# Forward and backward of a recurrent-memory transformer block: hand-laid buffers in one tile and stages that hand over inside each other's last steps

## The chip, the cores and the metric

The kernel runs on one core of a Trainium2 chip. The metric is the device time of one execution in microseconds (us). A core has five engines, each with its own instruction queue worked off in order: TensorE (PE, with its weight loads PEld), VectorE (DVE), ScalarE (ACT), GpSimd (POOL) and SyncE (SP). In this kernel SP does nothing but start DMAs, and POOL starts DMAs beside a few copies. An instruction can wait for events of other engines and of DMAs; everything behind it on its engine then waits too.

## The reference

A block with 2048 tokens of width D = 448 is computed, and the gradients of all its inputs. The attention part walks through 64 segments of 32 tokens in order; each segment also carries 8 memory rows, and the memory rows of its output are the next segment's memory, so that segments depend on each other.

```python
mem = mem0
for s in range(n_seg):                                  # 64 segments of 32 tokens
    h = concatenate([mem, x[32 * s:32 * s + 32]])       # 8 + 32 rows
    q, k, v = h @ Wq, h @ Wk, h @ Wv                    # 16 heads of 256
    p = softmax(where(mask, q @ k.T / 16, -1e9))
    o = (p @ v) @ Wo
    mem = o[:8]; outs.append(o[8:])

h  = x + attention(layernorm(x))
h2 = h + (silu(n @ w_gate) * (n @ w_up)) @ w_down       # n = layernorm(h), inner width F = 1792
out, vjp = jax.vjp(block, x, mem0, Wq, Wk, Wv, Wo, w_gate, w_up, w_down)
return out, *vjp(grad_out)
```

All inputs and outputs are bfloat16; sums are float32 in PSUM.

## The kernel before

Four stages run one after the other, each a function that issues its instructions in the order in which they are to run; the order within each engine's queue is the order of the code.

1. `forward_chain` (from L406): 64 steps, one for each segment, about 14.0 us each. A step projects K, Q and V (L471, L479), transposes K and Q (L485), computes scores, softmax and PV (L516 to L814) and the output projection (L600), and hands the memory rows to the next step. V's rows are moved to other partitions by copies or by DMAs on SP (`v_shift`; L667 is the DMA form). Beside its own segment a step works at a side task for the row tile of 128 tokens (four segments): `u1`, `u2`, `u3` are PE work, `e1`, `e3` evictions, `ut` a transpose, `et` the last reduction. In the last step `ff.load_first` asks for the gate and up weights (L895, L897, on POOL).
2. `ffn_phase`: 16 row tiles of 128 tokens, forward and backward of the FFN. `gate`, `up` and `dz` are products with the gate, up and transposed down weights (L996, L999), `down_mm` is L1050, `dh_mm` L1079; `turn_f`, `hn_turn`, `dout_turn` and `dh_out` are transposes on PE; `slope` and `grads` are DVE work, `dh_ln` is the LayerNorm gradient (DVE). `ff.load_rest` (L905 to L911) asks SP for the down weight, its transpose `WdT` and the transposed gate and up weights. The shape 448 is three and a half times 128: WdT's last DMA transpose takes the last 128 columns, and a further DMA (L909) copies their second 64 rows to the first 64 partitions. A steady tile takes 20.2 us.
3. `backward_chain`: 64 steps in the opposite order, about 14.6 us each: gradient of the outputs through Wo (L1191), scores' gradient (L1472 to L1482), outer products (L1494), products with the transposed V, K and Q weights (`w_pass`, L1218). `load_back` (L926) loads such a transposed weight by one DMA transpose on SP.
4. `tail_phase`: 22 phases of weight gradients. p = 0 and 1 (L1674) use `GO_all`, p = 2 to 5 `HN_all` (L1689), p = 6 to 21 the attention's weights. A phase's large operand is loaded two phases ahead (`load_phase`), from p = 6 on by 16 DMA transposes on SP (L1629). In the first two phases memory rows are loaded, transposed and stored again (`mem_turn`, L1657 to L1666).

The weights lie in one SBUF tile `Wall` of four parts; each stage places its own weights there. All other buffers come from tile pools that are opened and closed with their stage: `workA`, `stageA`, `wfwd` for the first, `workB`, then `workC`, `stageC`, then `tailA`, `workD`. A pool's space is given to the next stage's pools. PSUM has eight banks: stages 1 and 3 use six in rotation and two fixed ones, stages 2 and 4 eight in rotation (`psf` is a bank used as float32, `psh` as bfloat16).

Of the kernel before, what the change touches and what calls it, by code (L numbers as in the profile page):

```python
# [18 lines left out]
class _Prio:  # L19
# [5 lines left out]
    def crit(self):  # L25
        from contextlib import contextmanager

        @contextmanager
        def _cm():
            off = self.tc.cur_priority - self.next  # L30
            with self.tc.high_priority(offset=off):
                yield
                self.next = self.tc.cur_priority
        return _cm()

# [147 lines left out]
def run_all(k: _K):  # L183
# [89 lines left out]
    with tc.tile_pool(name="wfwd", bufs=1) as wf, \  # L273
            tc.tile_pool(name="psA", bufs=6, space=bass.MemoryType.PSUM) as psa, \
            tc.tile_pool(name="psS", bufs=1, space=bass.MemoryType.PSUM) as pss:
        k.pspool = psa
        k.s_ps = [pss.tile([P, 512], FP32, name=f"s_ps{i}") for i in range(2)]
        for i in range(2):
            nc.vector.memset(k.s_ps[i][:], 0.0)
        Wk_sb, Wq_sb, Wv_sb = [W[i].rearrange("p (c n) -> p c n", c=KC) for i in range(3)]  # L280
        Wo_sb = W[3][:, 0:MC * D].rearrange("p (c d) -> p c d", c=MC)
        NWIN = 8
        hA = wf.tile([P, KC, NWIN, SEG], BF16)
        memT_all = W[3][:, MC * D:KC * HD].rearrange("p (c s m) -> p c s m", c=KC, s=NSEG)
        k.memT_all = memT_all
        maskf = wf.tile([L, L], FP32)
        nc.gpsimd.memset(maskf[:], 0.0)
        nc.gpsimd.affine_select(out=maskf[:], in_=maskf[:], compare_op=ALU.is_ge, fill=-1e9 / k.scale,
                                base=0, pattern=[[-1, L]], channel_multiplier=1)
        nc.gpsimd.memset(maskf[0:M, :], 0.0)  # L290
        maskr = wf.tile([L, H // 2 * L], BF16)
        for hh in range(H // 2):
            nc.vector.tensor_copy(out=maskr[:, hh * L:(hh + 1) * L], in_=maskf[:])
        k.part = wf.tile([P, DP], FP32, name="part")
        k.partB = wf.tile([P, DP], FP32, name="partB")
        nc.vector.memset(k.part[:], 0.0)
        nc.vector.memset(k.partB[:], 0.0)

        with tc.tile_pool(name="workA", bufs=2) as work, tc.tile_pool(name="stageA", bufs=1) as stage:
            order = ExitStack()  # L300
            order.enter_context(tc.manual_schedule())
            DB = D // 4
            m0f = work.tile([P, DP], BF16, name="m0", tag="xtmp", bufs=2)
            m0 = m0f[0:M, :]
            nc.sync.dma_start(out=m0[:, 0:D], in_=MEM0)
            Xs = W[3][:, 0:NT * D].rearrange("p (t d) -> p t d", t=NT)
            XNs = W[3][:, NT * D:2 * NT * D].rearrange("p (t d) -> p t d", t=NT)
            xv = X2.rearrange("(t p) d -> p t d", p=P)
            xnv = XN.rearrange("(t p) d -> p t d", p=P)
            for q in range(4):  # L310
                nc.sync.dma_start(out=Xs[:, 4 * q:4 * q + 4, :], in_=xv[:, 4 * q:4 * q + 4, :])
            for Wt, Wsrc in ((Wk_sb, Wk2), (Wq_sb, Wq2), (Wv_sb, Wv2)):
                wv = Wsrc.rearrange("(a j p) n -> a p j n", a=2, j=2)
                for a in range(2):
                    nc.sync.dma_start(out=Wt[0:DB].rearrange("p (j a) n -> p j a n", a=2)[:, :, a, :], in_=wv[a])
            pm = ps1(BF16)
            for kc in range(KC):
                w0 = (kc % 2) * 2 * DB + (kc // 2) * DB
                nc.tensor.transpose(pm[0:DB, kc * M:(kc + 1) * M], m0[:, w0:w0 + DB], ident[0:M, 0:M])
            k.evac(hA[0:DB, :, 0, 0:M], pm[0:DB, 0:KC * M].rearrange("p (c m) -> p c m", m=M), "v")  # L320
            nc.scalar.copy(out=memT_all[0:DB, :, 0, :], in_=hA[0:DB, :, 0, 0:M])
            mv1 = small.tile([P, NT, 2], FP32, name="mv1", bufs=1)
            sd1 = small.tile([P, NT], FP32, name="sd1", bufs=1)

            def norm_rows(out, t):
                nc.vector.tensor_scalar(out=out, in0=Xs[:, t, :], scalar1=mv1[:, t, 0:1], scalar2=rstd1[:, t:t + 1],
                                        op0=ALU.subtract, op1=ALU.mult)

            def first_rows(t):
                xl = work.tile([P, DP], BF16, name="xload", tag="xload", bufs=1)  # L330
                norm_rows(xl[:, 0:D], t)
                return xl

            def norm_group(q):
                ts = range(4 * q, 4 * q + 4)
                for t in ts:
# [7 lines left out]
            def store_group(q):  # L344
                for t in range(4 * q, 4 * q + 4):
                    norm_rows(XNs[:, t, :], t)
# [60 lines left out]
def forward_chain(k: _K, hA, NWIN, Wq_sb, Wk_sb, Wv_sb, Wo_sb, maskr, work, stage, ff):  # L407
# [289 lines left out]
    for s in range(NSEG):  # L697
# [44 lines left out]
        if s == NSEG - 1:  # L742
            ff.load_first()
# [186 lines left out]
def ffn_phase(k: _K, W, ff, work, mv2, rstd2, srcs):  # L930
# [194 lines left out]
    for t in range(NT):  # L1125
        if t + 2 < NT:
            load(t + 2)
# [715 lines left out]
```

## Time and profile before

| | us |
|---|---|
| median of three runs (lowest to highest) | 3011.68 (2999.15 to 3012.10) |
| profiled execution | 3027.69 |
| its span, first to last instruction | 3025.9 |

The median comes from runs without the profiler; the profile is of another, single execution. Its page gives first the busy time of each engine and its share of the span, and then the span in 40 slices, each digit a tenth of busy time, with PE's granted clock and the DMA engines' share under it:

```profile
PE 2782.4 (92%) x44584; PEld 1532.9 (51%) x44584; DVE 1527.2 (50%) x3995; ACT 1175.6 (39%) x3087; POOL 737.2 (24%) x1388
...
PE   3999999999997899977999999999997999989998
...
PEclk7999999999999899987999999999998999999999
DMA  9334434334335853377556655655666999999996
```

A slice is 75.6 us. The forward stage fills slices 1 to 12, the FFN 13 to 17, the backward stage 18 to 30, the tail the rest. Two fives in the DMA line mean that the mean DMA engine was busy half of that slice.

### The profile page before, as it was taken

The numbers are of one execution on the slowest core, as the hardware profiler recorded it, in microseconds if no ns is written. First come the engines' busy times: TensorE is split into PE (matmuls) and PEld (weight loads), VectorE is DVE, ScalarE is ACT, GpSimd is POOL, SyncE is SP. The second block draws the span as 40 slices with busy tenths as digits, with TensorE's granted clock in tenths as the row PEclk, the third lists the DMA queues.
The fourth block names the chain that finished last, engine by engine and source line by source line (L and its number), as shares of the span: only waits on it lengthen the run. The fifth ranks groups of instructions, "written<-read, shape, count | busy, mean of one in ns | idle before, by whom it ended". The sixth has DMA issues, their size and how long they took to land.

```text
span 3025.9 us, 104914 instructions
## 1 busy us (share of the span) xinstructions
PE 2782.4 (92%) x44584; PEld 1532.9 (51%) x44584; DVE 1527.2 (50%) x3995; ACT 1175.6 (39%) x3087; POOL 737.2 (24%) x1388
## 2 busy tenths in 40 slices
PE   3999999999997899977999999999997999989998
PEld 1555555555554355544555555555554454444454
DVE  3566666666665577754555666555663111112121
ACT  2444445454453466543444444444542011111110
POOL 1222222222222122211222322222222223222231
PEclk7999999999999899987999999999998999999999
DMA  9334434334335853377556655655666999999996
GB/s 262 116 119 134 122 120 141 119 116 143 116 118 170 191 154 124 112 178 176 145 147 174 175 142 149 193 153 144 181 160 239 280 214 203 207 191 192 202 199 105
DMA packets 623699, 494.03 MB, mean 163 GB/s; under 512 B 486144, under 2 KB 535888, under 8 KB 613696
## 3 DMA queue, kind: packets, MB, share of 16 engines
q1 hardware_dynamic: 574848, 295.48, 44.5%
q0 software_dynamic: 48384, 191.85, 19.5%
q8 instruction: 352, 5.77, 0.8%
q14 instruction: 115, 0.94, 0.1%
HBM read 137.63 MB, written 222.08 MB: 119 GB/s over the span
## 4 chain that ended last, share of the span: by engine, by line
PE 71%; DVE 8%; DMA 7%; issue 6%; ACT 4%; SPq 2%; POOL 1%; another core or an unknown queue 0%; POOLq 0%; ACTq 0%; DVEq 0%
PE psf L1689 12%; PE psf L1218 9%; PE psf L471 8%; PE psf L1191 5%; PE psf L600 4%; PE psf L996 3%; PE psf L1494 3%; PE psf L1674 3%; PE psf L479 2%; PE psf L1079 2%; PE psh L485 2%; PE psf L1702 2%; PE psf L814 2%; DMA V_sb<-Vev 2%; DMA wall<-in_A_Wv_dram 1%
## 5 line engine op out<-in xcount | busy, mean ns | idle before, releaser
L1689 PE MATMUL psf<-wall,H_all 128*128 128x512 bf16 x1440 | 325.8, 384 | 15.4 <-DMA wall<-dKA 10.3
L471 PE MATMUL psf<-wall,hA 112*32 112x512 bf16 x4096 | 234.6, 381 | 3.5
L1689 PEld LDWEIGHTS <-H_all 128*128 128x128 bf16 x1440 | 140.2, 99 | 184.7 <-issue 29.9
L1601 DVE CAST resc<-psf 128x512 bf16<-128x512 f32 (+1 forms) x58 | 39.1, 673 | 324.7 <-PE psf L1689 290.6
L471 PEld LDWEIGHTS <-hA 112*32 112x32 bf16 x4096 | 104.4, 97 | 113.8 <-DVE hA L529 12.9
L1599 ACT CAST resc<-psf 128x512 bf16<-128x512 f32 (+1 forms) x54 | 31.0, 573 | 337.1 <-PE psf L1689 299.7
L1545 POOL COPY dmem<-dA 128x32 bf16<-128x32 bf16 x63 | 13.2, 210 | 558.9 <-DVE dA L1230 558.9
L437 POOL COPY V_sb<-Vev 32x512 bf16<-32x512 bf16 x128 | 77.2, 603 | 273.9 <-ACT Vev L434 270.2
L1182 DVE COPY partC<-psf 128x224 f32<-128x224 f32 x64 | 25.1, 392 | 227.1 <-ACT partC L1185 227.1
L1191 PE MATMUL psf<-wall,dA 128*32 128x512 bf16 x2048 | 123.7, 384 | 13.0 <-DVE dA L1230 13.0
L479 PE MATMUL psf<-wall,hA 112*32 112x512 bf16 x2048 | 134.0, 382 | 0.0
L1674 PE MATMUL psf<-dOut_all,wall 128*128 128x448 bf16 x640 | 127.3, 357 | 6.5 <-DMA wall<-OTA 6.5
L1674 PEld LDWEIGHTS <-wall 128*128 128x128 bf16 x864 | 84.4, 99 | 95.2 <-issue 13.2
L1218 PE MATMUL psf<-wall,dkA 128*32 128x448 bf16 x2048 | 116.9, 371 | 14.6 <-DMA wall<-in_A_Wk_dram 12.1
L1218 PE MATMUL psf<-wall,dqA 128*32 128x448 bf16 x2048 | 112.1, 359 | 14.9 <-DMA wall<-in_A_Wq_dram 10.4
L1218 PE MATMUL psf<-wall,dvA 128*32 128x448 bf16 x2048 | 124.3, 362 | 0.9 <-issue 0.6
L1182 DVE COPY dO_sb<-dOev 32x512 bf16<-32x512 bf16 x256 | 120.4, 470 | 7.0
L600 PE MATMUL psf<-wall,oA 128*32 128x224 bf16 x4096 | 115.3, 267 | 0.3
L1185 ACT CAST dOev<-psf 128x512 bf16<-128x512 f32 x64 | 37.4, 585 | 184.8 <-PE psf L1191 181.0
L1218 PE MATMUL pob<-wall 128*32 128x448 bf16 x1536 | 107.3, 359 | 1.1 <-issue 1.1
L1185 ACT CAST wall<-psf 128x64 bf16<-128x64 f32 x512 | 106.7, 247 | 0.0
L600 PEld LDWEIGHTS <-oA 128*32 128x32 bf16 x4096 | 97.0, 99 | 8.1
(285 smaller groups left out, 5803.9 us busy)
## 6 DMA issues: line engine op xcount, KB each, us to landing
Vtok<-V_sb SPq DMA_DIRECT2D x128, 192.0 KB
KtokA<-Kev SPq DMA_DIRECT2D x64, 256.0 KB
QtokA<-Qev SPq DMA_DIRECT2D x64, 256.0 KB
OTA<-oA POOLq DMA_DIRECT2D x16, 1024.0 KB, 5.4
Q_sb<-QtokA SPq DMA_DIRECT2D x128, 128.0 KB
K_sb<-KtokA SPq DMA_DIRECT2D x128, 128.0 KB
dVA<-dvA POOLq DMA_DIRECT2D x16, 1024.0 KB, 5.8
dKA<-dkA POOLq DMA_DIRECT2D x16, 1024.0 KB, 7.8
```

The lines of the kernel that those rows point to most:

```text
L437: nc.gpsimd.tensor_copy(out=out, in_=in_)
L471: nc.tensor.matmul(ps[32 * g:32 * g + 32, :], lhsT=stat(kc), rhs=W_sb[0:DB, kc, c0:c0 + HB], start=(kc == 0), stop=(kc == KC - 1))
L479: nc.tensor.matmul(ps[32 * g:32 * g + 32, :].rearrange("t (y d) -> t y d", y=2), lhsT=stat(kc), rhs=wv[:, x, :, half, e, :], start=(kc == ...
L600: nc.tensor.matmul(ps[32 * g:32 * g + 32, 0:2 * DB], lhsT=x, rhs=Wo_sb[:, c, a * 2 * DB:(a + 1) * 2 * DB], start=first, stop=last)
L996: nc.tensor.matmul(out[b][:, 0:BW], lhsT=xT[:, kc, :], rhs=Wx[:, kc, f0:f0 + BW], start=(kc == 0), stop=False)
L1182: nc.vector.tensor_copy(out=out, in_=in_)
L1185: nc.scalar.copy(out=out, in_=in_)
L1191: nc.tensor.matmul(ps[32 * g:32 * g + 32, :], lhsT=stat(kc), rhs=WoT_sb[:, kc, c0:c0 + HB], start=(kc == 0), stop=(kc == KC - 1))
L1218: nc.tensor.matmul(pO[32 * g:32 * g + 32, 0:D], lhsT=ch(c), rhs=WT[:, c, :], start=(first and i < 4), stop=(last and i >= MC - 4), skip_gr ...
L1494: nc.tensor.matmul(po[:, n * L:(n + 1) * L], lhsT=lhs[b:b + L, lc:lc + P], rhs=rhs[b:b + L, hh, 0:L], start=True, stop=True)
L1674: nc.tensor.matmul(ps[:, 0:D], lhsT=stat[:, i, c * P:(c + 1) * P], rhs=Y[:, i, 0:D], start=(i == 0), stop=(i == kts - 1))
L1689: nc.tensor.matmul(ps[:, 0:N], lhsT=Hx[:, i, dc * P:(dc + 1) * P], rhs=X[:, i, b * N:(b + 1) * N], start=(i == 0), stop=(i == kts - 1))
```

## The change

Five things change; the diff leaves out what is only indented anew.

- One SBUF tile of 77,824 bytes a partition, the arena, takes the place of all stage pools. Four texts (`FWD`, `FFN`, `BWD`, `TAIL`) give each buffer its offset and its number of copies; a stage's `tile()` returns a view and takes the copies in turn. An instruction then waits only for those that touch the same bytes.
- One PSUM pool of six rotating banks and two fixed ones (`k.fix`) stays open throughout. The FFN's `down_mm` and `dh_mm` use the fixed ones.
- The FFN, backward and tail functions become generators. `next(feed)` in the forward stage's last step runs the FFN up to its next `yield`, `next(back)` in the FFN runs a part of the backward stage's start, `next(tails)` in the backward stage's last step the tail's first loads.
- In the forward stage's last step the three V shifts by DMA become copies on ACT and POOL. `load_rest` asks for WdT's transposes ahead of the down weight; the copy of the 64 odd rows goes to POOL.
- The FFN takes its last two row tiles in the order 15, 14, with their work interleaved; the transposed V, K and Q weights are loaded in two pieces each. sg, u and z get two copies; `slope` writes its result over sg.

```diff
+class _Stage:
...
+    def tile(self, shape, dtype, name=None, tag=None, bufs=None):
+        tag = tag or name
+        offs = self.slots[tag]
+        i = self.count.get(tag, 0)
+        self.count[tag] = i + 1
+        off, nb = offs[i % len(offs)]
...
+        return self.arena.view(off, shape, dtype)
+ARENA = 77824
...
+FFN = """h_ld:896x3 hn:1024x3 dout_ld#2:1024x2 dh_t:1792 lnb_prod:1792 lnb_t1:1792 dh_b:896 o_t:896x2 dT:1024x2
+dout_ld#0:1024x2
+du:3584 dgp:3584 dz:3584 scr:3584
+sg#0:3584 g#0:3584 u#0:3584 sg#1:3584 g#1:3584 u#1:3584
+doutT:1024x2
+z:3584x2 hnT:1024x2"""
...
 def run_all(k: _K):
...
+    arena = _Arena(wtp.tile([P, ARENA // 2], BF16, name="arena")[:, :])
+    fwd, ffn, bwd, tail = [_Stage(arena, ARENA, text) for text in (FWD, FFN, BWD, TAIL)]
+    k.pspool = ctx.enter_context(tc.tile_pool(name="psA", bufs=6, space=bass.MemoryType.PSUM))
+    pss = ctx.enter_context(tc.tile_pool(name="psS", bufs=1, space=bass.MemoryType.PSUM))
+    k.fix = [pss.tile([P, 512], FP32, name=f"s_ps{i}") for i in range(2)]
...
+        tails = tail_phase(k, tail)
+        back = backward_chain(k, WT, bwd, bwd, rstd1, dmem0T, tails)
+        feed = ffn_phase(k, WT, ff, ffn, mv2, rstd2, {"o": Wo2, "v": Wv2, "k": Wk2, "q": Wq2}, back)
+        forward_chain(k, hA, NWIN, Wq_sb, Wk_sb, Wv_sb, Wo_sb, maskr, fwd, fwd, ff, feed)
         nc.gpsimd.dma_start(out=memTd[0:DB], in_=memT_all[0:DB].rearrange("p c s m -> p c (s m)"))
+        next(feed)
+        for _ in back:
+            pass
+        for _ in tails:
+            pass
...
 def forward_chain(k: _K, hA, NWIN, Wq_sb, Wk_sb, Wv_sb, Wo_sb, maskr, work, stage, ff, feed):
...
-        nc.sync.dma_start(out=dr["Hh"][t * P:(t + 1) * P, :], in_=h_t)
+        eng = nc.gpsimd if t == NT - 1 else nc.sync
+        eng.dma_start(out=dr["Hh"][t * P:(t + 1) * P, :], in_=h_t)
...
         v_b_rows(s, V_sb)
+        final = s == NSEG - 1
+        if final:
+            next(feed)
...
-        v_shift(V_sb, Vev, 0, (2, 3), D_)
+        v_shift(V_sb, Vev, 0, (2, 3), A if final else D_)
...
-        v_shift(V_sb, Vev, 1, (0,), D_)
+        v_shift(V_sb, Vev, 1, (0,), G_ if final else D_)
...
         p_ev(1, 1, V)
+        if final:
+            next(feed)
...
             nc.sync.dma_start(out=dr["Vtok"][s, gg], in_=V_sb[QB * gg:QB * gg + 48, :])
+        if final:
+            next(feed)
...
         late["ut"]()
+        if final:
+            uo = o_units(t)
+            uo["u1"]()
+            uo["u2"]()
+            uo["u3"]()
+            next(feed)
...
+    uo["e3"]()
+    next(feed)
+    uo["ut"]()
+    uo["et"]()
+    next(feed)
     out_pe(NT - 1)
     out_ev(NT - 1)
...
     def load_rest(self):
...
-        nc.sync.dma_start(out=self.Wd, in_=Wd2.rearrange("(c p) d -> p c d", p=P))
         for kc in range(full):
             nc.sync.dma_start_transpose(out=self.WdT[:, kc, :], in_=Wd2[:, kc * P:(kc + 1) * P])
         nc.sync.dma_start_transpose(out=self.WdT[:, full, :], in_=Wd2[:, D - P:D])
-        nc.sync.dma_start(out=self.WdT[0:rem, full, :], in_=self.WdT[P - rem:P, full, :])
+        nc.sync.dma_start(out=self.Wd, in_=Wd2.rearrange("(c p) d -> p c d", p=P))
         nc.sync.dma_start_transpose(out=self.WgT, in_=k.aps["B_w_gate"])
         nc.sync.dma_start_transpose(out=self.WuT, in_=k.aps["B_w_up"])
...
     def down_mm(t):
-        T[t].pf = ps1(FP32)
+        T[t].pf = k.fix[0]
...
-    def dh_mm(t):
-        T[t].pdh = ps1(FP32)
+    def dh_mm(t, parts=range(2)):
+        pdh = k.fix[1]
...
+    ORD = list(range(NT - 2)) + [NT - 1, NT - 2]
+    HC = k.MC // 2
     load(0)
     load(1)
-    ff.load_rest()
+    yield
     rstd(0, NT - 1)
     norm(0)
-    rstd(NT - 1, NT)
-    norm(1)
+    yield
+    ff.load_rest()
+    yield
     hn_turn(0)
-    gate(0)
+    yield
+    gate(0, (0,))
+    nc.gpsimd.dma_start(out=ff.WdT[0:rem, full, :], in_=ff.WdT[P - rem:P, full, :])
+    yield
+    gate(0, (1,))
+    yield
+    norm(1)
     up(0)
     dout_turn(0)
     hn_turn(1)
     slope(0)
...
+    for i in range(NT - 2):
+        t, n1, n2 = ORD[i:i + 3]
...
+        if i == NT - 6:
+            next(back)
...
+        if i == NT - 3:
+            dout_turn(n1)
+            hn_turn(n2)
+            gate(n2)
+            load_back(k, WT["v"], srcs["v"], False, 0, HC)
+            up(n2)
+            load_back(k, WT["v"], srcs["v"], False, HC, 2 * HC)
+            dh_turn(t)
+            slope(n1)
+            slope(n2)
...
+        dh_mm(t)
+    p, q = ORD[NT - 2:]
+    turn_f(T[p].z, ff.zT, (A, A))
+    dz(p)
+    dh_ln(p - 2)
+    down_mm(p)
+    grads(p)
+    dh_out(p - 2)
+    down_ev(p)
+    dout_turn(q)
+    turn_f(T[q].z, ff.zT, (A, A))
+    dz(q)
+    load_back(k, WT["k"], srcs["k"], False, 0, HC)
+    down_mm(q)
+    down_ev(q)
+    next(back)
+    load_back(k, WT["k"], srcs["k"], False, HC, 2 * HC)
+    dh_turn(p)
+    grads(q)
+    dh_mm(p)
+    dh_ln(p)
+    dh_turn(q)
+    dh_mm(q, (0,))
+    dh_out(p)
+    next(back)
+    load_back(k, WT["q"], srcs["q"], False, 0, 14)
+    dh_mm(q, (1,))
+    load_back(k, WT["q"], srcs["q"], False, 14, 2 * HC)
+    dh_ln(q)
+    yield
+    dh_out(q)
+    yield
...
 def backward_chain(k: _K, WT, work, stage, rstd1, dmem0T, tails):
...
+    load_vT(NSEG - 1)
+    load_vT(NSEG - 2)
+    yield
+    nc.vector.memset(S_ps[:], 0.0)
+    kq = load_kq(NSEG - 1)
+    Pn = load_P(NSEG - 1)
+    yield
     nc.gpsimd.memset(dA[:, :, slot(NSEG - 1), 0:M], 0.0)
     new_tile(NT - 1)
     open_tile(NT - 1)
     nc.gpsimd.memset(tiles[NT - 1].dmem[:, :, 3, :], 0.0)
     fill_tile(NT - 1)
+    yield
     u = do_units(NT - 1)
...
-            cur = w_units(t + 1, "v") if t + 1 < NT else none_units()
+            cur = w_units(t + 1, "v") if t + 1 < NT else dict(none_units(), u2=lambda: next(k.feed))
...
+            eng = nc.gpsimd if s == NSEG - 1 else nc.sync
...
         outer(K_sb, dST, dqA, T.dW["q"], (V, A, V, A))
+        if s == 0:
+            next(tails)
...
 def tail_phase(k: _K, work):
...
     load_rows(GO_all, GO2, 4)
+    yield
     load_phase(0)
     load_phase(1)
-    load_rows(HN_all, dr["HN"], 1)
...
             for i in range(NG):
                 box = {}
                 at(i, lambda box=box, m=mems[p * NG + i]: box.update(pe=mem_turn(*m)))
-                at(i + 2, lambda box=box: box["pe"]())
+                at(i + 3, lambda box=box: box["pe"]())
+        if p == 0:
+            HN_all = work.tile([P, NKT, D], BF16, name="HN_all", tag="h2")
+            load_rows(HN_all, dr["HN"], 1)
```

The memory tiles of `mem_turn` have five copies instead of two. `dh_out` of row tile 14 writes straight into the buffer that the backward stage reads, without a store and a load.

745 lines of the change are left out of this document (380 added, 365 removed).

## The prediction

> **What bounds the kernel now.** I read the stretches first: the whole span cut at the points where one stage hands over to the next. Columns: stretch, its length, busy time (instructions) of PE, weight load, DVE, ACT, POOL, then the granted clock, the DMA share and GB/s.
>
> ```profile
> 62.00:954.00 892.00, 854.30 (x17540) 496.54 (x17536) 556.31 (x1738) 433.28 (x1126) 212.25 (x454) 0.99 0.41 125
> 954.00:1023.40 69.40, 42.43 (x461) 21.55 (x458) 28.46 (x66) 26.17 (x51) 11.81 (x22) 0.80 0.90 240
> 1023.40:1312.80 289.40, 289.40 (x2040) 153.10 (x2040) 220.43 (x366) 172.75 (x294) 63.46 (x113) 0.99 0.43 130
> 1312.80:1382.50 69.70, 36.65 (x434) 19.14 (x431) 20.63 (x48) 16.40 (x37) 7.85 (x16) 0.68 0.90 211
> 1382.50:2291.00 908.50, 856.86 (x19676) 490.51 (x19680) 539.22 (x1436) 434.10 (x1423) 231.30 (x473) 0.99 0.59 158
> 2291.00:2376.80 85.80, 68.60 (x680) 35.46 (x681) 16.26 (x42) 13.40 (x35) 24.62 (x43) 0.92 0.87 307
> 2376.80:3025.90 649.10, 619.48 (x3649) 310.73 (x3647) 123.90 (x233) 71.00 (x104) 175.01 (x241) 0.98 1.05 194
> ```
>
> Inside a stage PE sets the pace: busy 94 to 100% at a clock of 0.98 or more. The three joints are different: 225 us together, PE idle for 77 of them and on a lowered clock for part of the rest, while the DMA share is 0.87 to 0.90. The change works there. PE's timeline (start, length, instructions; in brackets the idle time before it and what ended it) gives the waits:
>
> ```profile
> 967.89 0.43 PE L814 MATMUL psf<-PT,V_sb 104*128 104x80 bf16 x4 [4.50 <-DMA V_sb<-Vev]
> 985.01 0.58 PE L978 MATMUL psh<-ident,hn 128*128 128x128 bf16 x4 [5.77 <-DVE hn L970]
> 1005.72 0.55 PE L999 MATMUL psf<-wall,doutT 64*128 64x448 bf16 x2 [6.64 <-DMA wall<-wall]
> 1331.22 0.61 PE L1096 MATMUL psh<-ident,dh_b 128*128 128x128 bf16 x4 [3.92 <-DVE dh_b L946]
> 1363.60 3.18 PE L1218 MATMUL psf<-wall,dkA 128*32 128x448 bf16 x32 [12.15 <-DMA wall<-in_A_Wk_dram]
> 1377.18 3.18 PE L1218 MATMUL psf<-wall,dqA 128*32 128x448 bf16 x32 [10.40 <-DMA wall<-in_A_Wq_dram]
> 2323.60 4.56 PE L1674 MATMUL psf<-GO_all,wall 128*128 128x448 bf16 x12 [7.67 <-DMA memld<-memTd]
> ```
>
> What is late behind them stands in SP's timeline: a weight transpose holds SP's queue while it is issued.
>
> ```profile
> 985.55 10.43 SPq L907 DMA_TRANSPOSE wall<-in_B_w_down_dram  x3
> 1009.42 6.82 SPq L911 DMA_TRANSPOSE wall<-in_B_w_up_dram  x1
> 1346.65 14.53 SPq L926 DMA_TRANSPOSE wall<-in_A_Wk_dram  x1
> 1361.23 13.71 SPq L926 DMA_TRANSPOSE wall<-in_A_Wq_dram  x1
> ```
>
> The chain that ended last shows what a new pool's buffers waited for: the old pool's last stores.
>
> ```profile
> 1331.56 2.22 DMA DHb<-dh_b
> ...
> 2317.36 1.99 DMA out_dram<-dm
> ...
> 2321.32 7.00 DMA GO_all<-in_grad_out_dram
> ```
>
> **Joint 1, forward to FFN: 16 us.** In the last step three V shifts by DMA (L667), which land behind the gate and up weights, become two ACT copies and one POOL copy (0.62 and 0.63 us by rows of such copies). The waits of 4.50, 1.63 and 0.35 us on them go; ACT is later by 1.2 us ahead of its two exponentials and by 1.6 (table load 1.28, square root 0.31) ahead of its oA evictions. load(0) and load(1), six issues of 0.43 us, now stand on SP ahead of the K, Q and V stores, for which nobody waits in this step. load_rest (SP 985.08 to 1016.24) starts behind the V store, about 966. The shift of the 64 odd rows of WdT moves to POOL; behind it wait only stores, that of the last Hh row tile among them, needed 250 us later and, by its buffer, before hn_turn(1).
>
> Two sums for when dh_mm(0) starts (1023.36 now). PE: from 963.4, with lengths of the steady step and FFN tile, 1.5 (PV) + 3.4 (128 Wo matmuls) + 2.5 (lateness of ACT) + 1.6 (transposes) + 6.1 (gate, up) + 0.45 + 0.8 + 3.1 (dz) + 2.7 (down) + 6.1 (next gate, up) + 2.0 = 994, some 5 more for evictions and a cold clock: 999. DMA: from 956, 3.67 MB gate and up at the 310 GB/s of that stretch 11.8; three weights transposed, about 6.6 each by L910 and L911, 19.8; Wd 5.2; OTA, OTB and memT stores 5.5 at 268 GB/s; step stores 3; rows 2: 47.3, so 1003. Then h_ld(2), which SP issues behind WuT, 2 us, and the 2.3 from its landing to dh_mm (1021.11 to 1023.36): 1007.5. I take the later, a gain of 16. Bounds: 24 by PE's sum, 5 if only the V_sb stall less ACT's lateness goes.
>
> The Trainium skill bears on this ("DMA: Bandwidth & Descriptors", Issuing engines are not separate DMA queues): whichever engine starts a DMA, all run on the same 16 engines, so a second issuer saves issue time only. The share of 0.90 fits; by the rule the byte sum holds (16), without it PE's sum (24).
>
> **Joint 2, FFN to backward: 30 us.** Row tiles 15 and 14 change places, gate and up of both run ahead, so the last dh_ln (DVE 3.9 us, PE idle now) lies under other PE work, and WvT, WkT, WqT are cut into pieces that each start when their part of the weights is free. From turn_f(13) (1272.55 now) PE's work to the last dh_mm is 54.75 us now; in the new order the same instructions, plus about 0.7 where dh_mm(14) waits until dh_ln(15) has read the fixed bank (reads 1171.85 to 1173.80 in a steady tile, 1.95, less the 1.57 of dh_turn, plus latency). Backward then starts at 54.5 in place of 61.9 (1334.49). SP: WvT is through by about 37; the first half of WkT goes after dz(14) at 37.1. Halves of 14.53 cost 7.3, times 1.25 for the FFN's own share of 0.3: 46.2. load_kq, eight issues of 0.35: 49. Second half 58. WqT, 6.0 and 7.7: 72, landing 2.2 later (1374.95 to 1377.18): 74. In a steady step the WqT pass comes 11.1 after the step's start (2290.95, 2302.07); step 63 starts at 57.6 (do_units 3.1), so PE would want WqT at 68.7 and waits 5.3 in place of 12.15 + 10.40. Pass and turn 5.4: the next step starts at 79.4, where it is 109.96 now (1382.51): 30. Also moved to POOL: four dO_sb loads, 0.55 each, behind dOB at 57.1, landing about 62, when outer needs them. Bounds: 36 (WqT in time), 20 (pieces at twice their rows).
>
> **Joint 3, backward to tail: 16 us.** GO_all's four loads go into step 0 behind outer(K); SP has nothing else there but Zt. They no longer wait for the dm store and land before 2316, when PE ends the dmem0 transposes. p=0 and p=1 are 14 units of 3.03 us and 8 transposes of 0.22: 44.2, so p=2 starts at 2360 for 2376.8. HN_all moves behind the load of DGP; 14.6 MB (GO, Zt, HN, two DGP) at 370 GB/s are 39 us from about 2302, in time. A memory tile is asked for three units ahead, not two: about 7.9 us after the POOL issues, against 5.7 to 6.1 from issue to use (2336.51 to 2342.16, 2353.22 to 2359.27). Bounds: 18 and 10 (half the memory waits stay).
>
> **The FFN's six banks: minus 3 us.** The eight rotating banks become six, pf and pdh have fixed ones. In the steady tile before,
>
> ```profile
> 1184.23 2.21 DVE L1021 TENSOR_TENSOR z<-psf,g 128x448 bf16<-128x448 f32 x4
> 1186.31 0.39 PE L978 MATMUL psh<-ident,hn 128*128 128x128 bf16 x4
> ```
>
> the hn transposes would take the bank that the last z frees at 1186.44, 0.13 after PE wants it; all other allocations have 0.18 us or more. With latency 0.2 a tile, 13 tiles: 3. Bounds 0 and 6. Second buffers for sg, u and z, and two more table loads on ACT (1.28 each, under joint 1's DMA), cost nothing: DVE and ACT are busy 76% and 60% of that stretch. If DVE had no slack, each of z's 0.13 would be paid in full again.
>
> **What stays.** The arena only renames buffers: in the steady forward and backward steps the compiled order has the same instructions, waiting for the same engines. WdT's last 128-column transpose is in both kernels (L908); it is only issued before Wd. Cost 0; if wrong, see the second rival. The tail keeps its row: each load waits for PE to free its place, so an earlier start moves all of it.
>
> Sum 16 + 30 + 16 - 3 = 59. The profiled execution took 3027.69 (span 3025.9), 0.5% above the median of 3011.68; its sum gives 2969, the median less 59 gives **2953**.
>
> **The rivals.** (1) *DMA owns the joints.* The byte sum at joint 1 and SP's chain at joint 2 are stretched by what now overlaps; gains 5, 20 and 10 less 3: 32, so 2980. For: shares of 0.9. Against: 1.05 is held for 649 us in the tail. (2) *It does not do what it says*: views of one tile wait for each other in steady steps. 0.5 us in each of 127 steps eats 63: 3012, no change. Against: the wait lists.
> (3) *Slower.* With six banks PE pauses between matmul groups in the FFN and loses its clock. Cold matmuls in joint 2 cost 3.44 us for 32, warm 1.91: 1.8 times. At half of the 289 us that is 116 lost, 57 more than gained: 3069; it decides from a quarter of the FFN on. Against: the forward stage runs on six banks with 38 us of pauses at a clock of 0.99. The Trainium skill names such a case ("TensorE: Matmul & The Clock Gate", A second HAM failure mode): cycling through PSUM banks lets PE idle briefly and often enough that the clock falls and rises. This trace, at 0.99, does not show it.
>
> **Chances.** Forecast 0.62 (own range 2930 to 2975), DMA 0.23, no gain 0.08, slower 0.07. A difference under 0.5% (15 us) cannot be told from none: faster 0.85, same 0.08, slower 0.07. The range reaches up past the first rival and down to the better bounds of joints 1 and 2 (2953 - 8 - 6 - 2 - 3 = 2934, and a little for the runs' own spread of 13): 2928 to 2990.
>
> **What would show it.** L814 of the last forward step without a wait; the first dh_mm about 52 us after that step's start (69 now); the passes over WkT and WqT with at most 6 us of waits; the first tail unit right behind the dmem0 transposes; FFN tiles of 20.2 to 20.5 us. Wrong if joint 1 ends as late as before because WuT lands late, if a tile of the FFN grows past 21 us, or if the steady steps of 14.0 and 14.6 us change.

## The result and the profile after

| | before | changed |
|---|---|---|
| median of 18 runs each, us | 3011.89 | 2982.43 |
| lowest to highest | 2999.15 to 3031.89 | 2966.50 to 3007.83 |
| ratio, 95% interval | | 0.989 (0.987 to 0.991) |
| span of the profiled execution | 3025.9 | 3006.0 |

The change gains 29.5 us where 59 were forecast; by the interval it is 26 to 39 us. The forecast's sign holds, and so does its range of 2928 to 2990; its own narrower range, 2930 to 2975, does not. Half of its size is missing. One later run of the changed kernel, 4363.87 us at a granted clock of 0.557 where its other runs have 0.97 and more, is left out of every ratio here. The next table says where the time went. A stretch runs from one PE instruction's start in the timeline to another's: joint 1 from the last forward step's first projection (954.03 before, 952.00 changed) to the first matmul of `dh_mm`; the FFN from there to `turn_f(13)`; joint 2 from there to step 62; the chain to step 0; joint 3 from there to the tail's p=2. A second trace of the changed kernel, taken later, stands beside the first.

| stretch, us | before | changed | second trace | gain (first trace) | forecast |
|---|---|---|---|---|---|
| joint 1 | 69.3 | 77.1 | 87.1 | -7.7 | +16 |
| FFN | 249.2 | 250.5 | 250.8 | -1.3 | -3 |
| joint 2 | 110.0 | 86.9 | 87.6 | +23.0 | +30 |
| backward chain | 908.4 | 916.3 | 905.5 | -7.8 | 0 |
| joint 3 | 85.9 | 72.9 | 72.5 | +13.0 | +16 |
| tail | 649.1 | 650.4 | 633.4 | -1.3 | 0 |

The busy times of the changed kernel in its joint 1, FFN, joint 2 and joint 3, with the columns of the same view of before:

```profile
952.00:1029.10 77.10, 41.45 (x459) 22.91 (x458) 29.31 (x67) 28.59 (x53) 14.03 (x26) 0.78 1.07 215
1029.10:1279.50 250.40, 250.40 (x1758) 132.32 (x1757) 188.73 (x315) 149.44 (x255) 54.97 (x98) 0.99 0.43 134
1279.50:1366.50 87.00, 73.33 (x722) 39.18 (x723) 49.92 (x97) 41.08 (x79) 16.90 (x33) 0.90 0.90 212
2282.70:2355.60 72.90, 67.15 (x681) 35.56 (x682) 15.71 (x42) 13.41 (x35) 24.70 (x43) 0.95 1.01 356
```

In joint 1 PE does its 41 us of work in 77. The DMA share has risen from 0.90 to 1.07, but the rate has fallen from 240 to 215 GB/s: the DMA engines are busier and move less in each microsecond. Joint 3 shows the opposite, 0.87 to 1.01 with 307 to 356 GB/s. PE's largest waits in the joints of the changed kernel, from its timeline:

```profile
963.83 1.36 PE L890 MATMUL psf<-arena 104*128 104x80 bf16 x16 [1.73 <-DMA arena<-arena]
969.51 5.41 PE L668 MATMUL psf<-wall,arena 128*32 128x224 bf16 x128 [4.32 <-DVE arena L499]
1001.53 0.56 PE L1076 MATMUL psf<-wall,arena 64*128 64x448 bf16 x2 [14.98 <-DMA wall<-wall]
1026.78 1.65 PE L1114 MATMUL psh<-ident,arena 128*128 128x128 bf16 x14 [9.77 <-DVE arena L1099]
1345.36 0.74 PE L1607 MATMUL s_ps<-arena 128*40 128x40 bf16 x32 [3.01 <-POOL arena L1560]
1352.61 1.31 PE L1629 MATMUL psf<-arena 40*128 40x40 bf16 x32 [6.50 <-DMA arena<-arena]
2309.16 3.92 PE L1808 MATMUL psf<-arena,wall 128*128 128x448 bf16 x12 [2.26 <-DMA arena<-in_grad_out_dram]
```

The two waits for WkT and WqT of before (12.15 and 10.40) and the one for `memld` (7.67) have gone. The largest that is left is `dz(0)`'s: it waits 14.98 us for the odd rows of WdT, for which it waited 6.64 before. SP's and POOL's timelines of the same kernel show what happened in that time:

```profile
984.23 28.24 SPq L990 DMA_TRANSPOSE wall<-in_B_w_gate_dram  x1
1012.56 10.24 SPq L991 DMA_TRANSPOSE wall<-in_B_w_up_dram  x1
1022.85 0.57 SPq L1039 DMA_DIRECT2D arena<-Hh  x1
...
1338.86 18.78 SPq L1004 DMA_TRANSPOSE wall<-in_A_Wq_dram  x2
```

```profile
986.89 0.53 POOL L1204 DMA_DIRECT2D wall<-wall  x1 [15.42 <-PE psf L1073]
987.41 0.57 POOL L722 DMA_DIRECT2D Hh<-arena  x1
987.98 0.56 POOL L466 DMA_DIRECT2D memTd<-wall  x1
988.54 0.56 POOL L1050 DMA_DIRECT2D HN<-arena  x1
989.10 0.54 POOL L1100 DMA_DIRECT2D Zt<-arena  x1
```

The WgT transpose holds SP for 28.24 us where it held it for 6.39 before (L910, behind the same shift in SP's own queue, with no transfer of POOL's moving beside it). Some 4 us of that go with the load of Wd, which now stands ahead of it in the same queue (an experiment below, where POOL's transfers are not beside its start, has 10.7). It starts beside five POOL transfers that are released within 2.2 us: the shift L1204, for which POOL stood 15.42 us, and four stores behind it. The row puts that wait down to PE; in the second trace the same instruction waited 17.06 us, and there the row names the landing of WdT (`DMA wall<-in_B_w_down_dram`), which the shift reads. Behind WuT stands the load of tile 2's h (1022.85), and for that `norm(2)`, and with it DVE's queue and PE at 1026.78.

### The profile page after: what moved, and what is told of

It reads as the page before. It is cut to its first block, busy times and chain, and to the rows that moved or that the text cites. A ratio compares the mean times of both kernels' runs of the same rounds, so it can differ in the third digit from the quotient of the medians.

```text
span 3006.0 us, 104659 instructions
## 1 busy us (share of the span) xinstructions
PE 2775.5 (92%) x44584; PEld 1533.1 (51%) x44584; DVE 1525.6 (51%) x3994; ACT 1177.2 (39%) x3092; POOL 741.2 (25%) x1393
## 4 chain that ended last, share of the span: by engine, by line
PE 44%; DVE 5%; issue 3%; DMA 2%; ACT 1%; SPq 1%; POOL 0%; POOLq 0%; DVEq 0%; ACTq 0%
PE psf L1823 13%; PE psf L1343 9%; PE psf L1315 4%; PE psf L1808 3%; PE psf L1629 3%; PE psf L1836 2%; PE s_ps L1343 2%; PE s_ps L1607 2%; PE psf L1350 1%; PE psh L1321 1%; PE psh L1656 1%; DVE arena L1617 1%; DVE arena L1611 1%; DVE arena L1614 1%; DVE rsum L1613 1%
## 5 line engine op out<-in xcount | busy, mean ns | idle before, releaser
L1823 PE MATMUL psf<-wall,arena 128*128 128x512 bf16 (+1 forms) x1824 | 399.2, 377 | 19.8 <-DMA wall<-dQA 10.5
L502 ACT CAST arena<-psf 128x512 bf16<-128x512 f32 (+2 forms) x560 | 239.3, 452 | 372.1 <-PE psf L539 250.9
L1343 PE MATMUL psf<-wall,arena 128*32 128x448 bf16 x6144 | 341.2, 363 | 13.3 <-issue 13.0
L539 PE MATMUL psf<-wall,arena 112*32 112x512 bf16 x5120 | 309.7, 384 | 30.1 <-DMA wall<-in_A_Wk_dram 13.8
L1309 ACT CAST arena<-psf 128x256 bf16<-128x256 f32 (+1 forms) x593 | 231.9, 418 | 264.9 <-PE psf L1315 186.4
L1823 PEld LDWEIGHTS <-arena 128*128 128x128 bf16 x1824 | 177.1, 98 | 224.1 <-issue 34.7
L499 DVE CAST arena<-psf 128x512 bf16<-128x512 f32 (+2 forms) x432 | 189.7, 469 | 114.2 <-PE psf L539 84.4
L1306 DVE CAST arena<-psf 128x256 bf16<-128x256 f32 (+1 forms) x335 | 161.7, 483 | 74.2 <-PE psf L1629 41.9
L1808 PE MATMUL psf<-arena,wall 128*128 128x448 bf16 x864 | 172.4, 358 | 6.8 <-DMA wall<-OTA 3.9
L547 PE MATMUL psf<-wall,arena 112*32 112x512 bf16 x2560 | 169.2, 385 | 8.8 <-DMA wall<-in_A_Wv_dram 8.8
L1315 PE MATMUL psf<-wall,arena 128*32 128x512 bf16 x2560 | 160.9, 381 | 15.2 <-DVE arena L1355 14.9
```

Of the source, the lines that this page charges most:

```text
L499: nc.vector.tensor_copy(out=out, in_=in_)
L502: nc.scalar.copy(out=out, in_=in_)
L539: nc.tensor.matmul(ps[32 * g:32 * g + 32, :], lhsT=stat(kc), rhs=W_sb[0:DB, kc, c0:c0 + HB], start=(kc == 0), stop=(kc == KC - 1))
L547: nc.tensor.matmul(ps[32 * g:32 * g + 32, :].rearrange("t (y d) -> t y d", y=2), lhsT=stat(kc), rhs=wv[:, x, :, half, e, :], start=(kc == ...
L1306: nc.vector.tensor_copy(out=out, in_=in_)
L1309: nc.scalar.copy(out=out, in_=in_)
```

## The experiments

Theory A: plain transfers that POOL releases beside the weight transposes on SP make both crawl, and the shift's move to POOL is what brought them together. Rival B: joint 1 is simply bound by its bytes, in whatever order they go. All stretches below are from each run's own trace, as in the table above, one trace for each kernel but the changed one. Two traces with the code of before in joint 1 give 69.3 and 72.2 us for it (the second is the run with six banks), two with tile 2's loads early 51.5 and 52.8 (the second is the run for joint 2), so a difference of 3 us between two stretches says little. The time that WgT holds SP repeats better: 6.4 and 6.3 us in the first pair, 8.6 and 8.9 in the second. The time of the kernel before is that of its runs on the same chip.

### The shift back on SP

```diff
         nc.sync.dma_start_transpose(out=self.WdT[:, full, :], in_=Wd2[:, D - P:D])
+        nc.sync.dma_start(out=self.WdT[0:rem, full, :], in_=self.WdT[P - rem:P, full, :])
...
-    nc.gpsimd.dma_start(out=ff.WdT[0:rem, full, :], in_=ff.WdT[P - rem:P, full, :])
```

> The changed kernel with the odd rows' shift of WdT put back on SP, right behind the third WdT transpose; nothing else differs. Measured from the start of the last forward step to the first matmul of dh_mm (69.4 us before, 77.1 in the changed kernel). Theory A (the shift and the stores queued behind it on POOL run beside the WgT and WuT transposes on SP, and both crawl): the WgT and WuT issues go back from 28.2 and 10.2 us towards the 6.4 and 6.8 of before unless the stores alone suffice to slow them, the stretch falls to 52 to 64 us, and the kernel to 2957 to 2972 us. Rival B (the stretch is bound by the sum of the bytes, in whatever order they go): the stretch stays within 3 us of 77 and the time within 5 us of 2982. Rival C (the shift by itself is slow wherever it is put, since it goes from SBUF to SBUF): SP now waits about 10 us more in front of WgT, the stretch is 75 to 85 us.

Joint 1 took 67.3 us, WgT and WuT 10.7 and 9.5, the kernel 2974.4 (ratio 0.987, 0.983 to 0.990). Rival B is out: the same bytes, 9.8 us less. The stretch is above theory A's 52 to 64; SP stood 5.5 us for the landing of WdT before it could issue the shift (982.57 to 988.09), and PE waited 6.69 for it. Rival C is half right: on SP the shift costs a wait, but less than on POOL.

### The shift on DVE

```diff
-    nc.gpsimd.dma_start(out=ff.WdT[0:rem, full, :], in_=ff.WdT[P - rem:P, full, :])
...
     norm(1)
     up(0)
+    V(ff.WdT[0:rem, full, :], ff.WdT[P - rem:P, full, :])
```

> The changed kernel with the odd rows' shift done by a copy on DVE behind norm(1) and up(0), no DMA at all; the stores of Hh, memTd, HN and Zt stay on POOL. Theory A: the stretch from the last forward step to dh_mm (77.1 us) falls to 52 to 62 us if the copy from SBUF to SBUF is what slows the transposes; if any store beside them does, WgT still takes over 15 us to issue and the stretch stays above 68. Rival B (sum of the bytes): the shift is 224 KB of about 8 MB, so the stretch changes by under 3 us. DVE's copy of 64 x 1792 itself should take 1 to 4 us.

Joint 1 66.0 us, WgT and WuT 10.9 and 12.2, DVE's copy 0.62 us, less than the 1 to 4 expected; the kernel 2976.6 (0.985, 0.982 to 0.989). The stretch lies between the two that theory A allowed (52 to 62, or above 68). The 11.1 us against the first trace of the changed kernel are far more than rival B's 3. With nothing in front of them the stores leave POOL at 975.8 to 979.4, beside WdT's transposes and no longer beside WgT. So this run does not say what they cost beside WgT; a run below does.

### The stores behind WuT

The run before, and `memTd`, HN (tile 1) and Zt (tile 0) issued on SP after `load_rest`:

```diff
-        nc.gpsimd.dma_start(out=dr["Zt"][rows(t), :], in_=o.z[:])
+        (nc.sync if t == 0 else nc.gpsimd).dma_start(out=dr["Zt"][rows(t), :], in_=o.z[:])
```

> As the run with the shift on DVE, and the stores of memTd, HN (one tile) and Zt (one tile) that left POOL beside the transposes are issued on SP behind WuT instead. Theory A in its wide form (any plain transfer of another queue slows the transposes): WgT and WuT issue in 13 to 15 us together, as before, and the stretch is 50 to 58 us, shorter than in the run with the shift on DVE by over 5 us. Theory A in its narrow form (only the SBUF to SBUF copy): within 4 us of that run. Rival B: 74 to 80 us, as in the changed kernel. The whole kernel by the wide form 2955 to 2965 us, by rival B 2982.

Joint 1 60.4 us, 5.5 less than with the stores on POOL; WgT and WuT 10.7 and 9.1, more than the 13 to 15 together that were expected, at least in part since WgT's time here holds the 1.6 MB of Wd ahead of it in the same queue. The kernel 2976.2 (0.987, 0.985 to 0.989) is above the 2955 to 2965 expected and is not told apart from the two runs above, nor could 6 us be. The wide form of theory A asked for over 5 us less than the run before, which came, and for 50 to 58 us, which did not. What PE waits for last is now this:

```profile
1006.67 1.65 PE L1114 MATMUL psh<-ident,arena 128*128 128x128 bf16 x14 [8.30 <-DVE arena L1099]
```

### Before, with its shift on POOL

```diff
-        nc.sync.dma_start(out=self.WdT[0:rem, full, :], in_=self.WdT[P - rem:P, full, :])
+        nc.gpsimd.dma_start(out=self.WdT[0:rem, full, :], in_=self.WdT[P - rem:P, full, :])
```

> The kernel before with one line changed: the odd rows' shift is issued on POOL in place of SP, everything else as it was. Theory A: the transposes that stand beside it on SP take longer to issue than the 6.4 and 6.8 us of before (10 us or more together), the stretch from the last forward step to dh_mm grows from 69.4 to 75 to 85 us, and the kernel is 5 to 15 us slower than 3012. Rival B: the stretch stays within 3 us of 69.4 or falls by the shift's 3 us, and the time within 5 us of 3012.

A miss for theory A's sizes: joint 1 70.3 us (69.3 before), the kernel 3009.3 for 3015.7 (0.998, 0.995 to 1.001). The transposes beside it did get longer, 7.3 and 10.4 us for 6.4 and 6.8, but SP no longer waits for WdT's landing and issues WgT 43.6 us after the start of the last forward step, 5.4 earlier than before (49.0). The two about cancel: moving the shift alone is no loss in the old order. The loss needs something of what the change put around it.

### The shift alone, and the stores alone, held back

Two halves of the changed kernel's POOL queue. The first is the run with the stores behind WuT, with the shift on POOL as in the change:

```diff
+    nc.gpsimd.dma_start(out=ff.WdT[0:rem, full, :], in_=ff.WdT[P - rem:P, full, :])
...
-    V(ff.WdT[0:rem, full, :], ff.WdT[P - rem:P, full, :])
```

> The changed kernel with the shift on POOL as the change has it, but memTd, HN (one tile) and Zt (one tile) issued on SP behind WuT, so that POOL has only the shift and the 112 KB store of Hh beside the WgT transposes. Against the run that differs from it in the shift alone (copy on DVE, same stores behind WuT: last forward step to dh_mm 60.4 us, WgT and WuT issued in 10.7 and 9.1 us). Theory A1 (the copy from SBUF to SBUF beside the transposes is what slows them): the stretch is 70 to 78 us, WgT takes over 20 us to issue. Theory A2 (it is the sum of held transfers, 1.4 MB released at one moment beside the transposes): the stretch is 60 to 66 us, WgT under 15 us.

The second is the run with the shift on DVE, with POOL's queue held until WdT has landed:

```diff
+    held = smal.tile([P, 2], BF16, name="held")
+    nc.gpsimd.tensor_copy(out=held[P - rem:P, :], in_=ff.WdT[P - rem:P, full, 0:2])
```

> The shift done by a copy on DVE, no transfer for it; but POOL waits for the last WdT transpose as it does in the changed kernel, by a copy of two columns, before it issues the stores of Hh, memTd, HN and Zt, so that these are released together beside the WgT transposes. Against the run with the shift on DVE and free stores (stretch 66.0 us, WgT and WuT 10.9 and 12.2 us). Theory A1 (the SBUF to SBUF copy): the stretch stays at 63 to 69 us. Theory A2 (1.1 MB of stores released at one moment beside the transposes): the stretch is 71 to 78 us and WgT takes over 18 us to issue.

Both cost: the shift, with the 112 KB store of Hh behind it, 8.5 us (68.9 for 60.4), the held stores alone 4.6 (70.6 for 66.0). WgT took 18.4 and 24.6 us to issue, 10.7 and 10.9 in the runs that they are compared with. Neither form of the theory is right by itself; the first run lies nearer A1, the second in A2's bounds but for 0.4 us. The DMA view of a stretch behind the release gives the rate; first the shift alone (983 to 996), then the held stores (990 to 1006), then the changed kernel (985 to 1012):

```profile
DMA packets 3821, 1.92 MB, mean 147 GB/s; under 512 B 2785, under 2 KB 3757, under 8 KB 3821
```

```profile
DMA packets 2894, 1.94 MB, mean 121 GB/s; under 512 B 2430, under 2 KB 2656, under 8 KB 2893
```

```profile
DMA packets 6833, 4.18 MB, mean 155 GB/s; under 512 B 4768, under 2 KB 6560, under 8 KB 6832
```

The first and the last of these windows open with the end of Wd's load. In the run with the shift alone the parts can be told apart: while Wd's plain load ran (981.5 to 986) the rate was 324 GB/s, and of the shift, issued at 981.89, hardly anything had moved (0.01 MB); from 986 to 995, with the WgT transpose and the shift both moving, it was 87; then, with the shift done, the transpose went on at some 290.

The times of these kernels, 2987.8 (0.990, 0.987 to 0.993) and 2985.8 (0.989, 0.984 to 0.994), are the changed kernel's again.

### A store in the shift's place

```diff
-    nc.gpsimd.dma_start(out=ff.WdT[0:rem, full, :], in_=ff.WdT[P - rem:P, full, :])
+    nc.gpsimd.dma_start(out=dr["oddrows"], in_=ff.WdT[P - rem:P, full, :])
```

> The run with the shift alone on POOL (stretch 68.9 us, WgT issued in 18.4 us, WuT in 7.6), with its transfer replaced by a store of the same 64 rows of 3.5 KB of WdT to DRAM that nobody reads, at the same place on POOL; the shift itself is a copy on DVE. If the target in SBUF is what makes the transposes crawl: WgT in 9 to 12 us, as with no transfer there at all (10.7), and the stretch 59 to 62 us. If any transfer released at the start of the WgT transpose does it: WgT in 15 to 20 us; the stretch then 60 to 66 us, since nobody waits for the store itself.

WgT 14.2 us, between the 10.7 without any transfer there and the 18.4 with the shift; joint 1 65.6 us; one timed run, 2967.9. So a store of the same rows to DRAM, here too with the store of Hh behind it, slows the transpose too, if less. That the shift's target lies in SBUF is not the condition, but it may be a part of the size; one trace of each does not settle that.

### Tile 2's loads ahead of WgT

The run with the stores behind WuT, and `load(2)` between Wd and WgT:

```diff
+        mid()
         nc.sync.dma_start_transpose(out=self.WgT, in_=k.aps["B_w_gate"])
...
-    ff.load_rest()
+    ff.load_rest(lambda: load(2))
```

> The run with the shift on DVE and the stores behind WuT, and the three loads for row tile 2 (h, dout) issued on SP between the load of Wd and the WgT transpose instead of behind WuT. Theory: in that run PE's last wait before dh_mm (8.3 us, on DVE, whose queue stands at norm(2), which waits for h of tile 2 behind WuT on SP) goes; what is left is WuT's own landing, so the stretch from the last forward step to dh_mm falls from 60.4 to 53 to 57 us, and the kernel to 2965 to 2972 us. Rival: the wait is WuT's landing in any case (the last transpose ends 2.6 us before the loads are issued), the stretch stays at 58 to 61 us.

Joint 1 51.5 us, 8.9 less, a little better than the 53 to 57 expected; the kernel 2962.4 (0.983, 0.979 to 0.987). The rival falls. PE's last waits there:

```profile
1004.67 1.22 PE L1115 MATMUL psh<-ident,arena 128*128 128x128 bf16 x14 [0.30 <-DVE arena L1100]
1010.60 2.81 PE L1157 MATMUL s_ps<-wall 128*128 128x448 bf16 x14 [1.61 <-DMA wall<-in_B_w_up_dram]
```

The 8.30 are down to 0.30. `dh_mm(0)` starts before WuT has landed, because its first 14 matmuls read WgT only; the second 14 wait 1.61 for WuT.

### Joint 2: dO_sb ahead of WqT

The run before, with step 63's `dO_sb` loads on SP and both WqT pieces behind them:

```diff
-            eng = nc.gpsimd if s == NSEG - 1 else nc.sync
-            eng.dma_start(out=dO_sb[QB * gg + SEG:QB * gg + L, g2 * GF:(g2 + 1) * GF],
+            nc.sync.dma_start(out=dO_sb[QB * gg + SEG:QB * gg + L, g2 * GF:(g2 + 1) * GF],
...
+        if s == NSEG - 1:
+            load_back(k, WT["q"], k.srcs["q"], False, 0, 14)
+            load_back(k, WT["q"], k.srcs["q"], False, 14, MC)
```

> As the run with tile 2's loads early, and in the joint from FFN to backward step 63's four loads of dO_sb go on SP, and both WqT transposes are issued on SP behind them; nothing else runs beside them. In the changed kernel they were issued on POOL at 1342.73 beside WqT, and PE waited 6.50 us for them at 1352.61. Theory A (plain transfers beside another queue's transposes crawl, here too): the four loads land within 3 us of their issue, the 6.5 us wait falls under 1.5 us, WqT lands some 4 us later and its pass waits 0 to 4 us; turn_f(13) to step 62 falls from 87 to 81 to 85 us. Rival (WqT's own landing bounds this joint): the stretch stays at 86 to 90 us and PE waits for WqT instead.

The waits for `dO_sb` are gone, but joint 2 is 86.3 us, 1.3 less than in the run before it: here the rival holds. SP's and PE's timelines:

```profile
1315.31 16.49 SPq L1005 DMA_TRANSPOSE wall<-in_A_Wq_dram  x2
```

```profile
1334.21 2.43 PE L1344 MATMUL psf<-wall,arena 128*32 128x448 bf16 x24 [6.58 <-DMA wall<-in_A_Wq_dram]
```

PE waits 6.58 us for WqT in place of 6.50 for `dO_sb`: here the joint ends with WqT. But this run also issues WqT later, behind the four loads (62.7 us after `turn_f(13)`, 59.3 in the changed kernel), so it does not show what the joint takes with the loads early and WqT where it was. The kernel took 2958.5 (0.980, 0.975 to 0.985); its interval lies below the changed kernel's, so this version, which differs in joint 1 above all, beats both. It isn't told apart from the run before it.

### Six banks in the kernel before

```diff
-        ... tc.tile_pool(name="psF", bufs=8, space=bass.MemoryType.PSUM) as psf:
+        ... tc.tile_pool(name="psF", bufs=6, space=bass.MemoryType.PSUM) as psf, \
+                tc.tile_pool(name="psG", bufs=1, space=bass.MemoryType.PSUM) as psg:
...
-        T[t].pf = ps1(FP32)
+        T[t].pf = k.fix[0]
...
-        T[t].pdh = ps1(FP32)
+        T[t].pdh = k.fix[1]
```

> The kernel before with the FFN's eight rotating PSUM banks cut to six, pf and pdh in two fixed banks, as the change has them; nothing else. By the prediction a tile of the FFN is 0.2 us longer, 13 tiles 2 to 3 us; the two traces so far show 1.3 (dh_mm(0) to turn_f(13) 249.2 before, 250.5 after). If the six banks are the cause: 250 to 252 us here, and 3012 to 3019 for the kernel. If they are not: 249.2 within 0.5.

The FFN's stretch is 250.3 us, as in the changed kernel and 1.2 more than before. The stretch by itself would not prove it: with eight banks it is 249.2 and, in the run with the shift on POOL, 247.5, and in the ten traces with the changed kernel's FFN 249.2 to 251.0, since its first tile differs from trace to trace. The step from one `dh_mm` to the next does: it is 20.18 us in both traces with eight banks (1247.07 to 1267.25 in the first) and 20.31 in this run and in all ten others with six, tile after tile. And the 0.13 us stand where the prediction put them, ahead of the hn transposes:

```profile
1281.11 0.39 PE L980 MATMUL psh<-ident,dout_ld 128*128 128x128 bf16 x4
1281.46 0.38 PE L980 MATMUL psh<-ident,hn 128*128 128x128 bf16 x4
```

They start 0.35 us after the dout transposes, 0.23 with eight banks (1266.80 and 1267.03). The banks are the cause. In the whole kernel it can't be seen: 3014.2 for 3012.8 (1.000, 0.997 to 1.003).

### The changed kernel once more

> The changed kernel once more, for a second trace of it. If the stretch from the last forward step to dh_mm is set by the mix of transfers, it is again 73 to 80 us (77.1 in the first trace; 69.4 before); FFN to backward 86 to 88, backward to tail 72 to 74. If the backward chain (916 us in the first trace, 908 before) and the tail (650, 649) vary by themselves, they come out anywhere from 899 to 916 and from 620 to 651.

The ratio to the kernel before is again 0.990 (0.986 to 0.993). Joint 1 is even longer than in the first trace, 87.1 us, above the 73 to 80 expected:

```profile
1010.98 0.56 PE L1076 MATMUL psf<-wall,arena 64*128 64x448 bf16 x2 [20.69 <-DMA wall<-wall]
```

WgT held SP for 31.6 us. The mix and its order are the same, its cost varies by 10 us. The DMA view from 991 to 1020 has a mean of 132 GB/s. The other joints repeat to 0.7 us. The backward chain and the tail vary by themselves. The ten traces of kernels with the changed kernel's code there and the three with the code of before overlap: 899 to 916 against 908 to 914 us for the chain, 628 to 651 against 620 to 649 for the tail. In the tail of the first trace the chain that ended last has two loads of `dKA` in it, 4.56 and 9.74 us; such stops differ from trace to trace.

## Why the prediction was right in its sign and wrong in its size

**Joint 1 (forecast +16, measured -7.7).** This is the step that failed, in two places. It said of the shift: "behind it wait only stores", and cost its move at nothing. And it priced "three weights transposed, about 6.6 each by L910 and L911", rows beside which no transfer of POOL's moved. In the changed kernel that row's operation took 28.24 us, since the shift and the stores that waited behind it came out beside it. The forecast asked who waits for the held stores (nobody) and not what they collide with when they are let go. The runs divide the loss, each by one trace and against the shorter of the changed kernel's two: taking the shift off POOL's queue gives 11.1 us (77.1 to 66.0), the stores 5.5 (to 60.4), tile 2's loads 8.9 (to 51.5). The last was in the sum, with 4.3 us. It gave twice that: in the run where it was taken away the loads also stood behind three stores, 2.5 us, and with them early `dh_mm` no longer waits for all of WuT. With all three mended the joint takes 51.5 us, 17.9 less than before, where the forecast had 53.5. It isn't a proof of the byte sum: WuT was waited for until 55.9 us after the step's start (1010.60 less 954.70), where the sum had it landed at 49; `dh_mm` starts earlier only because half of it doesn't need WuT. Even in that run `load_rest` begins 18.5 us after the step's start (973.17 less 954.70), where the prediction had it at 12 (966), and WdT, WgT and WuT hold SP for 11.5, 8.6 and 9.0 us, 29 where the sum had 19.8. A smaller slip in the same sum: the stores of OTA, OTB and memT are 1.77 MB by the profile's list of issues, 6.6 us at 268 GB/s and not 5.5.

Of the prediction's own signs, the first `dh_mm` 52 us after the step's start came only in the mended run; in the changed kernel its sign of being wrong came, a joint that ends as late as before or later, since tile 2's h is asked for behind WuT.

The V_sb part was right in the main: the waits of 4.50, 1.63 and 0.35 us on V_sb have become one of 1.73, where the forecast had none; it is for the DMA of other rows of V (L732), which the change leaves on SP. But PE then waits 4.32 us for DVE, whose queue stands at `norm(0)` for the h of tile 0; the sums had no term for that.

The rule weighed there, the Trainium skill's "DMA: Bandwidth & Descriptors", Issuing engines are not separate DMA queues, says that a second issuer saves issue time and no more. In this case the choice of the issuer was worth more: with the shift issued by POOL the joint was 9.8 us longer than with the same shift issued by SP (77.1 against 67.3), because it also decides what is held and what is let go beside what. In the order of before the same choice was worth 1.0 us (70.3 against 69.3). The same page of the Trainium skill (Queues, rings and completion order) says that each DMA engine takes turns between the queues packet by packet; by that alone the two streams would share the rate of one, about 290 GB/s in the steady slices of a transpose here, and not fall to 155, 147 and 121 together, as they did here.

**Joint 2 (forecast +30, measured +23.0 and, in the second trace, +22.4).** The mechanism was right: the pieces start as their place comes free, backward's first projection starts 56.9 us after `turn_f(13)` (54.5 forecast), and the WkT wait is gone. WqT was mis-sized: 13.7 us by the row of before, 18.78 measured beside POOL's `dO_sb` loads, 16.49 with those out of the way. The `dO_sb` loads were forecast to be issued 57 us after `turn_f(13)` and to land at 62, when they are needed. POOL issued them at 63.2 and they landed at 73.0; PE waited 6.50 us for them, and 3.01 for the copy L1560 that stands behind them on POOL. With them on SP and ahead of WqT both waits are gone, but the joint gains only 1.3 us, since PE then waits for WqT. How much of that is WqT's own and how much the loads put ahead of it stays open.

**Joint 3 (forecast +16, measured +13.0 and +13.4).** Right but for one sentence, that GO_all's loads land before PE ends the dmem0 transposes. PE waits 2.26 and 0.67 us for them, 2.9 of the missing 3.

**The FFN (forecast -3, measured -1.3).** Right in kind and in place, shown by the run with six banks. A tile is longer by 0.13 us, just the time by which the prediction saw the bank come free too late; the latency that it added, up to 0.2 a tile, did not come.

**The steady steps (0).** Held as far as traces can tell; the chain's -7.8 in the first trace is +3.0 in the second.

**The sum.** The four terms are 27.0 us in the first trace, against 29.5 between the medians. That they agree so well is luck: in the second trace, with joint 1 at 87.1, the same terms are 16.5. The time lands on the first rival (2980), but not by its parts: it had +5, +20, +10 and -3. That the range holds is luck in the same way: it reaches past 2975 only because it was drawn out to take in that rival, and the rival has joint 1 better than before, not worse. Its idea, that what overlaps stretches the transfers, was the right one for joint 1 and too mild there. The second rival (waits in every step) and the third (PE's clock in the FFN, 0.99 before and after) did not come. The version with joint 1 in order gains 53.7 us (2962.4 for 3016.2), near the 59 forecast for the change.

## What to carry to other kernels

A transfer that is moved to another queue must be priced where it lands: what is held behind it, when that is let go, and what runs on the DMA engines at that moment. A duration taken from a row where an operation had little beside it was only a lower bound here: WgT's 6.4 us became 8.6 at best and 31.6 at worst in the order of the change. And in a joint, what the next stage's first instruction waits for goes ahead of the weights that are needed later: three small loads behind two transposes cost 9 us here.

## What the runs showed of the hardware

That two queues together can move less than one alone was not expected. A weight transpose with nothing of POOL's moving beside it ran at 290 GB/s here (the WgT of before, 1006 to 1010). With the shift or the held stores released at the start of WgT, both together ran at 121 to 155 GB/s in the windows of 13 to 27 us above, and at 87 in the plainest stretch (the shift alone, 986 to 995). But it isn't so for every mix. In the run with tile 2's loads early, POOL's 0.92 MB of DGP and DU stores fall into the change from WgT to WuT (993 to 1006):

```profile
DMA packets 10490, 3.58 MB, mean 275 GB/s; under 512 B 10360, under 2 KB 10360, under 8 KB 10488
```

There the transposes all but stopped from 997.9 to 999.1, as they also do between WgT and WuT of before, where nothing of POOL's moves (67 GB/s from 1010.5 to 1012.4). They ran on for 0.7 us; then, from 999.6 to 1001.6, the stores went through, 0.80 MB of POOL's queue beside 0.08 MB of SP's at 440 GB/s together, and the transposes went on at 290. What separates the two kinds of mix stays open: the place in the transpose, the source and target of the plain transfer, and its size were not varied one by one.
